# Two small matmul loops turned inside out, and the first two tiles of a projection interleaved, in a fused attention and MLP kernel

## The chip, the cores and the metric

The kernel runs on one core of one Trainium2 chip. The metric is the device time of one execution in microseconds (us). Runs count as fast or slow (slow here: over 1.5% above the fastest of the same kernel). One execution of each kernel is also taken by the hardware profiler, and its trace gives a start time for every instruction. PE is TensorE (matmuls), DVE is VectorE, ACT is ScalarE, POOL is GpSimd, SP issues DMAs.

## The reference, cut to what matters

```python
xn = layernorm(x)                                  # x: 2048 tokens x 1024
out = x + A(xn, mem0, Wq, Wk, Wv, Wo) + B(xn, w1, w2, w3, w4)

def B(x):                                          # the MLP branch
    h = gelu(layernorm(x) @ w1)
    ...                                            # shifts, w2, w3, w4

def A(x, mem0):                                    # 64 segments of 32 tokens, 8 memory rows
    for s in range(64):
        h = concat(mem, x[segment s])
        q, k, v = h @ Wq, h @ Wk, h @ Wv           # 32 heads of 128
        o = softmax(mask(q k^T / sqrt(128))) @ v @ Wo
        mem = o[:8]
        out.append(o[8:])
```

The kernel does not run the 64 segments one after another. It takes each segment's next memory from averages ("psvb" and "psG" below), computes all segments at once, and checks at the end that this was close enough; otherwise a serial branch recomputes.

## The kernel before

Three places matter. First, the start: tokens come in tiles of 128; a tile is normalised by VectorE, transposed on TensorE (the first ones) or by DMA (tile 4 and from tile 6 on), and multiplied by w1. The contraction has eight slices `k` of 128; w1 arrives in four loads of two slices each.

```python
load_x(0); load_x(1); load_w1(0); load_w1(2); load_x(2); load_w1(4); load_w1(6)
...
def w1_first(ks):                                  # tile 0: slice by slice, as w1 arrives
    for k in ks:
        for co in range(KT):
            nc.tensor.matmul(first[:, co // 4, co % 4, :], w1_sb[:, k, co * P:(co + 1) * P], xn2Ts[0][:, 0, k, :],
                             start=(k == 0 and co % 4 == 0), stop=(k == KT - 1), skip_group_check=True)

def single(n, b):                                  # other tiles: output by output
    ps = mm_tile("ps1")[:].rearrange("p (c t) -> p c t", c=4)
    for c in range(4):
        co = 4 * b + c
        for k in range(KT):
            nc.tensor.matmul(ps[:, c, :], w1_sb[:, k, co * P:(co + 1) * P], xn2Ts[n // 2][:, n % 2, k, :], ...)
    gelu4(n, b, ps)
...                                                # the order of issue
pe_trans(0); ln_half(1, 1)
w1_first(range(5))
load_segone(); load_eye9(); ln_half(2, 0); ln_apply(1)
pe_trans(1)
w1_first(range(5, KT))
for b in range(2): gelu4(0, b, first[:, b, :, :])
ln_half(2, 1); ln_apply(2)
single(1, 0); pe_trans(2); normalise_x(0); single(1, 1)
...
for g in range(2, NT // 2):                        # from tile 4 on, two tiles at a time, 256 columns
    for n in nxt:                                  # the next two tiles: 6 and 7 while 4 and 5 are multiplied
        ...
        ln_apply(n)
        dma_trans(n)                               # DMA transpose, issued by SP
    stage1(g, range(4))
    ...
    stage1(g, range(4, KT))
```

Second, eight small projections of averages (psvb, 63 columns) beside a third small product that is not touched (psG, 63 columns).

```python
MZ = cpool.tile([P, KT, NZ], BF16)                 # NZ = 71: rows 142 bytes apart
vbT = cpool.tile([P, H, NG], BF16)                 # NG = 63: rows 126 bytes apart
xb = spec.tile([P, KT, NG], BF16)
...
ps = aux_tile([P, 4, NG], "A", "psvb")
for hh in range(4):
    for k in range(KT):
        nc.tensor.matmul(ps[:, hh, :], w[:, k, hh * P:(hh + 1) * P], xb[:, k, :], start=(k == 0), stop=(k == KT - 1))
...                                                # psG: hh outer, k inner, output psG[:, k, :], moving operand vbT[:, c * 4 + hh, :]
```

Third, sixteen small projections of the memories (psM, 71 columns).

```python
def mem_proj(s, nm, dst):
    w = A[nm, s.i]
    ps = mm_tile("psM")
    p3_ = ps[:, 0:4 * NZ].rearrange("p (h z) -> p h z", h=4)
    for hh in range(4):
        for k in range(KT):
            nc.tensor.matmul(p3_[:, hh, :], w[:, k, hh * P:(hh + 1) * P], MZ[:, k, :], start=(k == 0), stop=(k == KT - 1))
    nc.scalar.copy(dst[:, hsl(s.hg), :], p3_)
```

In each matmul the second operand is the stationary one (the weights) and the third is the moving operand, which is streamed past it column by column.

Of the kernel before, what the change touches and what calls it, by code (L numbers as in the profile page):

```python
# [21 lines left out]
P = 128  # L22
S = 2048
D = 1024
KT = D // P
# [38 lines left out]
def kernel(  # L64
# [16 lines left out]
    nc = tc.nc  # L81
# [45 lines left out]
    MZ = cpool.tile([P, KT, NZ], BF16)  # L127
# [6 lines left out]
    def mm_tile(name):  # L134
        return psum.tile([P, 512], F32, tag="mm", bufs=4, name=name)

    def aux_tile(shape, tag, name):
        return psum.tile(shape, F32, tag=tag, bufs=1, name=name)
# [6 lines left out]
    xb = spec.tile([P, KT, NG], BF16)  # L145
# [18 lines left out]
    with ExitStack() as keepx:  # L164
# [6 lines left out]
        with ExitStack() as p0:  # L171
            big = p0.enter_context(tc.tile_pool(name="p0big", bufs=1))
            ring = p0.enter_context(tc.tile_pool(name="p0ring", bufs=3))
            w1_sb = big.tile([P, KT, D], BF16)
# [26 lines left out]
            def ln_half(n, c):  # L201
                if c == 0:
                    sts[n] = ring.tile([P, 2, 6], F32, tag="st", name="st")
                nc.vector.bn_stats(sts[n][:, c, :], xts[n][:, c * 512:(c + 1) * 512])
                if c == 0:
                    return
                nc.vector.bn_aggr(lnst[:, n, 0:2], sts.pop(n)[:])
                ab = ring.tile([P, 2], F32, tag="ab", name="ab")
                nc.vector.tensor_scalar(ab[:, 0:1], lnst[:, n, 1:2], EPS, None, op0=ALU.add)
                nc.vector.tensor_scalar(ab[:, 1:2], ab[:, 0:1], EPS, lnst[:, n, 1:2], op0=ALU.mult, op1=ALU.add)  # L210
                nc.gpsimd.tensor_tensor(lnst[:, n, 2:4], ab[:], neghalf[:], op=ALU.pow)
                for t in {0: (3,), 1: (4, 5), 2: (6, 7)}.get(n, (n + 5,)):
                    if t < NT:
                        load_x(t)

            def ln_stats(n):
                ln_half(n, 0)
                ln_half(n, 1)

            xn2Ts = {}  # L220
# [3 lines left out]
            def ln_apply(n):  # L224
                g, j = divmod(n, 2)
                if j == 0:
                    xn2Ts[g] = ring.tile([P, 2, KT, P], BF16, tag="xn2T", name="xn2T", bufs=4)
                xn2 = xn2s[n] = ring.tile([P, D], BF16, tag="xn2", name="xn2", bufs=4)
                nc.vector.tensor_scalar(xn2[:], xts[n][:], lnst[:, n, 0:1], lnst[:, n, 3:4], op0=ALU.subtract, op1=ALU.mult)
                nms[n] = ring.tile([P, 1], F32, tag="nm", name="nm", bufs=8)  # L230
                nc.gpsimd.tensor_scalar(nms[n][:], lnst[:, n, 0:1], lnst[:, n, 2:3], -1.0, op0=ALU.mult, op1=ALU.mult)
# [11 lines left out]
            def normalise_x(n):  # L243
                nc.scalar.activation(xts[n][:], xts[n][:], ACTF.Identity, bias=nms.pop(n)[:], scale=lnst[:, n, 2:3])

            def pe_trans(n):
                xn2 = xn2s.pop(n)
                ps = [mm_tile("psT")[:], mm_tile("psT")[:]]
                for h in range(2):
                    p3_ = ps[h].rearrange("p (k t) -> p k t", k=4)  # L250
                    for k in range(4):
                        nc.tensor.matmul(p3_[:, k, :], xn2[:, (4 * h + k) * P:(4 * h + k + 1) * P], ident[:], start=True, stop=True)
                    for q in range(0, 4, 2 if n == 0 else 4):
                        w = 2 if n == 0 else 4
                        nc.scalar.copy(xn2Ts[n // 2][:, n % 2, 4 * h + q:4 * h + q + w, :], p3_[:, q:q + w, :])
# [14 lines left out]
                for co in cos:  # L270
                    w1_part(g, co, mm_tile("ps1")[:, 0:256], range(KT))

            first = aux_tile([P, 2, 512], "B", "ps1")[:].rearrange("p b (c t) -> p b c t", c=4)

            def w1_first(ks):
                for k in ks:
                    for co in range(KT):
                        nc.tensor.matmul(first[:, co // 4, co % 4, :], w1_sb[:, k, co * P:(co + 1) * P], xn2Ts[0][:, 0, k, :],
                                         start=(k == 0 and co % 4 == 0), stop=(k == KT - 1), skip_group_check=True)

            def gelu4(n, b, ps):
                nc.scalar.activation(hTB[:, 4 * b:4 * b + 4, 2 + n * P:2 + n * P + P], ps, ACTF.Gelu_apprx_tanh)

            def single(n, b):
# [4 lines that stand above are left out]
                        nc.tensor.matmul(ps[:, c, :], w1_sb[:, k, co * P:(co + 1) * P], xn2Ts[n // 2][:, n % 2, k, :], start=(k == 0), stop=(k == KT - 1))  # L289
                gelu4(n, b, ps)  # L290
# [4 lines left out]
            ln_apply(0)  # L295
            pe_trans(0)
            ln_half(1, 1)
            w1_first(range(5))
            load_segone()
            load_eye9()  # L300
            ln_half(2, 0)
            ln_apply(1)
            pe_trans(1)
            w1_first(range(5, KT))
            for b in range(2):
                gelu4(0, b, first[:, b, :, :])
            ln_half(2, 1)
            ln_apply(2)
            single(1, 0)
            pe_trans(2)  # L310
            normalise_x(0)
            single(1, 1)
            ln_stats(3)
            ln_stats(4)
            ln_apply(3)
# [36 lines left out]
        with ExitStack() as p2:  # L352
            ring = p2.enter_context(tc.tile_pool(name="p2ring", bufs=4))
            for n in range(NT):
                x1 = ring.tile([P, D], F32, tag="x1", bufs=6)
                st = ring.tile([P, 2, 6], F32, tag="st")
                for ch in range(2):
                    ps = mm_tile("ps2")
# [25 lines left out]
    with ExitStack() as p3:  # L384
# [3 lines left out]
        for c in range(7):  # L388
            t = big.tile([P, 4, D], BF16, name=f"w4_{c}")
# [23 lines left out]
        def use_chunk(c):  # L413
            t = chunks.pop(c)
            if c < 8:
                w = t[:].rearrange("p (k e) -> p k e", k=KT)
                ps = aux_tile([P, 4, NG], "A", "psvb")
                for hh in range(4):
                    for k in range(KT):
                        nc.tensor.matmul(ps[:, hh, :], w[:, k, hh * P:(hh + 1) * P], xb[:, k, :], start=(k == 0), stop=(k == KT - 1))  # L420
                vb = vbT[:, c * 4:(c + 1) * 4, :]
                nc.vector.tensor_scalar(vb, ps[:], 1.0 / L, None, op0=ALU.mult)
                sq = ring.tile([P, 4, NG], F32, tag="sq", bufs=1, name="sq")
                nc.gpsimd.tensor_tensor(sq[:], vb, vb, op=ALU.mult)
                for hh in range(4):
                    if c == 0 and hh == 0:
                        nc.gpsimd.tensor_copy(thr[:], sq[:, 0, :])
                    else:
                        nc.gpsimd.tensor_tensor(thr[:], thr[:], sq[:, hh, :], op=ALU.add)
                if c == 7:  # L430
                    nc.gpsimd.tensor_scalar(chk[:, NV + 7:2 * NV], thr[:], TOL2, None, op0=ALU.mult)
                    nc.gpsimd.tensor_copy(chk[:, NV:NV + 7], chk[:, NV + 7:NV + 8].to_broadcast((P, 7)))
                return
            c -= 8
            w = t[:].rearrange("p (h d) -> p h d", h=4)
            if c == 0:
                psG[0] = aux_tile([P, KT, NG], "B", "psG")
            for hh in range(4):
                for k in range(KT):
                    nc.tensor.matmul(psG[0][:, k, :], w[:, hh, k * P:(k + 1) * P], vbT[:, c * 4 + hh, :],  # L440
                                     start=(c == 0 and hh == 0 and k == 0), stop=(c == 7 and hh == 3), skip_group_check=True)
            if c == 7:
                nc.vector.tensor_copy(MZ[:, :, M:NZ], psG[0][:])
# [100 lines left out]
        for tb in range(4):  # L544
            for f in range(FT):
                ps = mm_tile("ps3")
# [12 lines left out]
            for j in range(4):  # L559
                n = tb * 4 + j  # L560
# [3 lines left out]
                for ch in range(2):  # L564
                    ps = mm_tile("ps4")
# [20 lines left out]
    def hsl(hg):  # L586
        return slice(4 * hg, 4 * hg + 4)
# [53 lines left out]
    def mem_proj(s, nm, dst):  # L641
        w = A[nm, s.i]
        ps = mm_tile("psM")
        p3_ = ps[:, 0:4 * NZ].rearrange("p (h z) -> p h z", h=4)
        for hh in range(4):
            for k in range(KT):
                nc.tensor.matmul(p3_[:, hh, :], w[:, k, hh * P:(hh + 1) * P], MZ[:, k, :], start=(k == 0), stop=(k == KT - 1))  # L647
        nc.scalar.copy(dst[:, hsl(s.hg), :], p3_)

    def mem_cols(s):  # L650
# [191 lines left out]
    for i in range(NS):  # L842
        s = new_step(i)
        p = steps.get(i - 1)
# [72 lines left out]
        if last:  # L917
            b = s.b
# [35 lines left out]
    with tc.If(cond > 0):  # L954
        with ExitStack() as fctx:
# [17 lines left out]
            with tc.For_i(0, NSEG, 1) as i:  # L973
# [7 lines left out]
                for hg in range(8):  # L981
# [8 lines left out]
                    ps = fps.tile([P, 4, L], F32, tag="mm")  # L990
# [4 lines left out]
                    ps = fps.tile([P, 4, L], F32, tag="mm")  # L995
# [4 lines left out]
                    ps = fps.tile([P, 512], F32, tag="mm")  # L1000
# [33 lines left out]
                for ch in range(2):  # L1034
                    ps = fps.tile([P, 512], F32, tag="op")
# [44 lines left out]
```

## Time and profile before

| | before |
|---|---|
| time, median of 6 | 1503.70 us (1503.56 to 1504.64) |
| span of the profiled execution | 1502.0 us |
| PE busy | 1486.4 us, 99% |
| PE waits in the whole run | four, the last ends at 12.7 us |

The page of the kernel before, its busy times and the chain of work that ended last:

```profile
PE 1486.4 (99%) x9330; PEld 785.5 (52%) x9456; DVE 666.7 (44%) x1561; ACT 467.4 (31%) x1247; POOL 258.1 (17%) x707
...
PE 98%; DMA 1%; issue 0%; SPq 0%; DVE 0%
```

The waits of PE in the kernel before (who waited for whom: total us, times, longest):

```profile
PE ps L278 <- DMA w_sb<-in_B_w_dram: 1.5, 2, 0.9
PE psW L197 <- DVE fill L176: 1.5, 1, 1.5
PE psT L252 <- DVE xn L229: 1.2, 1, 1.2
PE ps L278 <- ACT xn2T L255: 0.2, 1, 0.2
```

PE is the bound, and after the start it never waits. So time can come from two places only: a shorter distance between the starts of matmuls, or the waits of the start-up. (After the last matmul come another 4.6 us, which the change does not touch.) The time order of PE in the kernel before (start, length, instruction; L278 is `w1_first`, L252 a transpose, L289 `single`; in brackets the idle time ahead and what ended it):

```profile
7.78 1.95 PE L278 MATMUL ps<-xn2T,w_sb 128*128 128x128 bf16 x32 [0.24 <-ACT xn2T L255]
10.64 0.62 PE L278 MATMUL ps<-xn2T,w_sb 128*128 128x128 bf16 x8 [0.92 <-DMA w_sb<-in_B_w_dram]
11.10 0.61 PE L252 MATMUL psT<-c_ident_sb,xn 128*128 128x128 bf16 x8
11.54 0.61 PE L278 MATMUL ps<-xn2T,w_sb 128*128 128x128 bf16 x8
12.71 1.07 PE L278 MATMUL ps<-xn2T,w_sb 128*128 128x128 bf16 x16 [0.56 <-DMA w_sb<-in_B_w_dram]
...
26.07 1.19 PE L265 MATMUL ps<-xn2T,w_sb 128*128 128x256 bf16 x9
```

Read it as: tile 0's first four slices, a wait for w1's third load, a transpose of tile 1, another wait for w1's fourth load. The first 128x256 matmul (L265, tiles 4 and 5) ends what is called the start-up below. The same view around the first psM group:

```profile
528.89 1.28 PE L647 MATMUL psM<-MZ,w 128*128 128x71 bf16 x32
530.01 2.32 PE L615 MATMUL psQ<-xm,w 128*128 128x512 bf16 x9
```

The lengths there include the last matmul's own latency (0.2 us), so the cost of a group is read from start to start: 530.01 - 528.89 = 1.12 us for 32 matmuls, 34.9 ns each. Single start times in the trace split this further: 31 to 32 ns after one matmul of each run of eight, 35 to 38 ns after the other seven.

### The profile page before, as it was taken

To read this page: it belongs to the slowest core of one execution; us is meant where nothing else is said; L and a number is where in the kernel's file an instruction comes from. 1 tells how busy PE (TensorE), PEld (TensorE's weight loads), DVE (VectorE), ACT (ScalarE), POOL (GpSimd) and SP (SyncE) were. 2 spreads that over 40 slices of the span, in tenths; PEclk is the share of its full clock that TensorE was granted. 3 is DMA by queue.
4 is the path that set the end of the run, shared out by engine and by line. 5 is a ranking of instruction groups with operands and counts; after the bars stand their busy time and mean duration, and the time that the engine had idled before them with its cause. 6 is when DMAs were issued, how large, how long until landed. Compare 5 with 4: busy or idle time off the path is not lost.

```text
span 1502.0 us, 23719 instructions
## 1 busy us (share of the span) xinstructions
PE 1486.4 (99%) x9330; PEld 785.5 (52%) x9456; DVE 666.7 (44%) x1561; ACT 467.4 (31%) x1247; POOL 258.1 (17%) x707
## 2 busy tenths in 40 slices
PE   8999999999999999999999999999999999999998
PEld 7844444444444466666644544444544544444544
DVE  8283010010110226666622777731676650576654
ACT  5633203103012035454501444420434430244420
POOL 6152131211110202121210111110111110111110
PEclk9999999999999999999999999999999999999999
DMA  7499753553121545474521454431455441344302
GB/s 223 131 276 219 269 186 99 184 175 132 63 92 42 197 136 188 142 224 141 183 71 61 140 168 141 155 103 49 141 152 158 141 132 58 104 138 141 118 0 72
DMA packets 189172, 208.11 MB, mean 139 GB/s; under 512 B 50168, under 2 KB 157832, under 8 KB 189056
## 3 DMA queue, kind: packets, MB, share of 16 engines
q1 hardware_dynamic: 180768, 178.82, 39.8%
q0 software_dynamic: 8288, 27.72, 5.2%
q8 instruction: 76, 1.25, 0.4%
q14 instruction: 40, 0.33, 0.1%
HBM read 170.07 MB, written 25.17 MB: 130 GB/s over the span
## 4 chain that ended last, share of the span: by engine, by line
PE 98%; DMA 1%; issue 0%; SPq 0%; DVE 0%
PE psK L631 15%; PE psQ L615 15%; PE psP L811 15%; PE psV L638 15%; PE ps L549 13%; PE ps L567 13%; PE ps L361 4%; PE ps L265 3%; PE psO L690 2%; PE psS L660 2%; PE psM L647 1%; PE ps L289 1%; DMA w_sb<-in_B_w_dram 1%; PE psvb L420 1%; PE psG L440 1%
## 5 line engine op out<-in xcount | busy, mean ns | idle before, releaser
L811 PE MATMUL psP<-wo_sb,oX 128*128 128x512 bf16 (+1 forms) x1036 | 221.7, 372 | 1.1
L664 ACT ACTIVATE ET<-psS 32x132 f32<-32x132 f32 x512 | 139.0, 271 | 203.7 <-PE psS L660 198.0
L567 PE MATMUL ps<-w,hT_all 128*128 128x512 bf16 x874 | 193.7, 379 | 1.2
L631 PE MATMUL psK<-xT,w 128*128 128x512 bf16 x747 | 176.3, 379 | 1.1
L615 PE MATMUL psQ<-xT,w 128*128 128x512 bf16 x750 | 175.8, 379 | 1.1
L638 PE MATMUL psV<-w,xT 128*128 128x512 bf16 x745 | 175.0, 379 | 1.0
L811 PEld LDWEIGHTS <-oX 128*128 128x128 bf16 x1056 | 102.8, 98 | 115.8
L631 PEld LDWEIGHTS <-w 128*128 128x128 bf16 x1280 | 121.2, 98 | 80.2
L550 ACT ACTIVATE hT_all<-ps 128x512 bf16<-128x512 f32 x112 | 66.7, 597 | 283.9 <-PE ps L549 283.9
L615 PEld LDWEIGHTS <-w 128*128 128x128 bf16 x1024 | 96.7, 98 | 104.2
L567 PEld LDWEIGHTS <-hT_all 128*128 128x128 bf16 x896 | 87.1, 98 | 103.9
L681 POOL TENSOR_TENSOR BD<-ET,c_segone_sb 128x16 bf16<-128x16 f32 x128 | 33.9, 265 | 491.1 <-ACT ET L664 491.1
L622 DVE TENSOR_TENSOR Q<-psQ,QM 128x512 bf16<-128x512 f32 (+1 forms) x128 | 85.6, 679 | 61.6 <-ACT Q L621 40.5
L638 PEld LDWEIGHTS <-xT 128*128 128x128 bf16 x768 | 72.0, 98 | 73.5
L666 DVE STREAM_TRANSPOSE EQ<-ET 128x128 f32<-128x128 f32 x128 | 39.9, 311 | 156.8 <-ACT ET L664 156.6
L639 ACT CAST V<-psV 128x512 bf16<-128x512 f32 x128 | 75.1, 586 | 110.1 <-PE psV L638 100.1
L632 ACT CAST K<-psK 128x512 bf16<-128x512 f32 (+1 forms) x160 | 80.3, 502 | 90.7 <-PE psK L631 88.9
L549 PE MATMUL ps<-xn3T,w3a 128*128 128x512 bf16 x448 | 97.7, 379 | 0.0
L549 PE MATMUL ps<-xn3T,w3b 128*128 128x512 bf16 x448 | 97.7, 379 | 0.0
L817 DVE TENSOR_TENSOR ot<-psP,Rt 128x512 bf16<-128x512 f32 (+1 forms) x33 | 22.2, 675 | 157.3 <-PE psP L811 157.3
L679 DVE TENSOR_TENSOR BD<-PT,c_segone_sb 128x512 bf16<-128x512 bf16 x128 | 90.0, 703 | 4.5
L694 DVE TENSOR_TENSOR oX<-psO,VM 128x512 bf16<-128x512 f32 (+1 forms) x128 | 86.3, 674 | 7.8 <-PE psO L690 7.8
(157 smaller groups left out, 1502.5 us busy)
## 6 DMA issues: line engine op xcount, KB each, us to landing
w<-in_A_Wq_dram SPq DMA_DIRECT2D x32, 1024.0 KB, 5.4
w<-in_A_Wk_dram SPq DMA_DIRECT2D x32, 1024.0 KB, 5.5
w<-in_A_Wv_dram SPq DMA_DIRECT2D x32, 1024.0 KB, 5.4
R_scratch<-x POOLq DMA_DIRECT2D x16, 512.0 KB, 7.9
R<-R_scratch SPq DMA_DIRECT2D x16, 512.0 KB, 7.1
chunk<-in_A_Wv_dram SPq DMA_DIRECT2D x8, 1024.0 KB, 5.6
R_scratch<-R POOLq DMA_DIRECT2D x16, 512.0 KB, 4.1
chunk<-in_A_Wo_dram SPq DMA_DIRECT2D x8, 1024.0 KB, 5.9
```

Of the source, the lines that this page charges most:

```text
L549: nc.tensor.matmul(ps[:], w3[:, k, (f % FH) * P:(f % FH + 1) * P], xn3Ts[tb][:, :, k, :], start=(k == 0), stop=(k == KT - 1))
L567: nc.tensor.matmul(ps[:], h3T[:, f, j * P:(j + 1) * P], w4t[f // 4][:, f % 4, ch * 512:(ch + 1) * 512], start=(f == 0), stop=(f == FT - 1))
L615: nc.tensor.matmul(ps[:], w[:, k, hh * P:(hh + 1) * P], s.xm[:, k, 0:512], start=(k == 0), stop=(k == KT - 1))
L622: nc.vector.tensor_tensor(q3[:, j0:16, 0:SEG], p3_[:, j0:16, :], QM[:, 4 * s.hg + hh, z + j0:z + 16].unsqueeze(2).to_broadcast((P, 16 - j0 ...
L631: nc.tensor.matmul(ps[:, 0:c], w[:, k, hh * P:(hh + 1) * P], s.xm[:, k, h2 * c:(h2 + 1) * c], start=(k == 0), stop=(k == KT - 1))
L632: nc.scalar.copy(s.K[:, hh, h2 * c:(h2 + 1) * c], ps[:, 0:c])
L638: nc.tensor.matmul(ps[:], s.xm[:, k, m * P:(m + 1) * P], w[:, k, :], start=(k == 0), stop=(k == KT - 1))
L639: nc.scalar.copy(s.V[:, m, :], ps[:])
L664: nc.scalar.activation(ET[q, :, :], ps[q, :, W * j:W * (j + 1)], ACTF.Exp, scale=SCALE)
L679: nc.vector.tensor_tensor(B4[:, :, :, 0:SEG], PT[:].unsqueeze(2).to_broadcast((P, 4, 4, SEG)), so.unsqueeze(3).to_broadcast((P, 4, 4, SEG) ...
L694: nc.vector.tensor_tensor(oX[:, hsl(s.hg), m * P:(m + 1) * P].rearrange("p h (j i) -> p h j i", i=SEG)[:, :, j0:4, :], p4[:, :, j0:4, 0:SE ...
L811: nc.tensor.matmul(ps[:, 0:w], oX[:, h, m * P:(m + 1) * P], wo_sb[:, h, cc], start=(h == 0), stop=(h == H - 1))
```

## The change

The intent: (1) in psvb and psM, go through the four heads inside the loop over the contraction, so that two consecutive matmuls never add to the same columns of PSUM, the memory in which TensorE sums; (2) at the start, put tile 1's first slices of w1 between those of tile 0, so that PE has work while w1 is still arriving.

The flag `start` has to move as well. The Trainium skill, "PSUM — Partial Sum Buffer", section "The four PSUM rules", says that a matmul with this flag clears the written-bits (which decide between adding and overwriting) of its whole bank, so that where several groups are open at once in a bank only the first matmul issued there may carry it. The new loops follow this.

```diff
-            w1_first(range(5))
+            w1_first(0, range(4))
             load_segone()
             load_eye9()
             ln_half(2, 0)
             ln_apply(1)
             pe_trans(1)
-            w1_first(range(5, KT))
-            for b in range(2):
-                gelu4(0, b, first[:, b, :, :])
+            w1_first(0, range(4, 6))
+            w1_first(1, range(3))
+            w1_first(0, range(6, KT))
             ln_half(2, 1)
             ln_apply(2)
-            single(1, 0)
+            w1_first(1, range(3, 6))
             pe_trans(2)
+            w1_first(1, range(6, KT))
             normalise_x(0)
-            single(1, 1)
 ... (w1_first takes the tile as an argument, keeps one PSUM tile for each, and issues the gelus after slice 7)
-                for hh in range(4):
-                    for k in range(KT):
-                        nc.tensor.matmul(ps[:, hh, :], w[:, k, hh * P:(hh + 1) * P], xb[:, k, :], start=(k == 0), stop=(k == KT - 1))
+                for k in range(KT):
+                    for hh in range(4):
+                        nc.tensor.matmul(ps[:, hh, :], w[:, k, hh * P:(hh + 1) * P], xb[:, k, :], start=(k == 0 and hh == 0),
+                                         stop=(k == KT - 1), skip_group_check=True)
 ... (mem_proj, psM: the same exchange of the two loops)
```

More of the change, by code (lines that the diff above doesn't have):

```diff
@@ L271, in stage1, with w1_first @@
                     w1_part(g, co, mm_tile("ps1")[:, 0:256], range(KT))
-            first = aux_tile([P, 2, 512], "B", "ps1")[:].rearrange("p b (c t) -> p b c t", c=4)
-            def w1_first(ks):
+            first = {}
+            def w1_first(n, ks):
+                if n not in first:
+                    first[n] = aux_tile([P, 2, 512], "BA"[n], "ps1")[:].rearrange("p b (c t) -> p b c t", c=4)
                 for k in ks:
                     for co in range(KT):
-                        nc.tensor.matmul(first[:, co // 4, co % 4, :], w1_sb[:, k, co * P:(co + 1) * P], xn2Ts[0][:, 0, k, :],
+                        nc.tensor.matmul(first[n][:, co // 4, co % 4, :], w1_sb[:, k, co * P:(co + 1) * P], xn2Ts[0][:, n, k, :],
                                          start=(k == 0 and co % 4 == 0), stop=(k == KT - 1), skip_group_check=True)
+                if ks[-1] == KT - 1:
+                    for b in range(2):
+                        gelu4(n, b, first[n][:, b, :, :])
             def gelu4(n, b, ps):
@@ L644, in mem_proj @@
         p3_ = ps[:, 0:4 * NZ].rearrange("p (h z) -> p h z", h=4)
-        for hh in range(4):
-            for k in range(KT):
-                nc.tensor.matmul(p3_[:, hh, :], w[:, k, hh * P:(hh + 1) * P], MZ[:, k, :], start=(k == 0), stop=(k == KT - 1))
+        for k in range(KT):
+            for hh in range(4):
+                nc.tensor.matmul(p3_[:, hh, :], w[:, k, hh * P:(hh + 1) * P], MZ[:, k, :], start=(k == 0 and hh == 0),
+                                 stop=(k == KT - 1), skip_group_check=True)
         nc.scalar.copy(dst[:, hsl(s.hg), :], p3_)
```

## The prediction

> **What bounds the kernel now.** TensorE. The page has PE busy 1486.4 of 1502.0 us (99%); the chain that ended last is 98% PE. The table of waits lists four PE waits in all, before 13 us: 1.5 us for the fill tile, 1.2 for the first normalised tile, 0.2 for ScalarE, 1.5 in two waits for w1's loads. Only shorter matmul pitches and those start-up waits can pay.
>
> **Part 1: small matmuls, contraction outermost.** 512 matmuls of 128x71 (psM) and 256 of 128x63 (psvb) change order. By start-to-start times in the trace, inside a run of eight that accumulates into the same columns psM has 35 to 36 ns, but 31 to 32 ns where the next matmul goes to another head's columns; a group of 32 takes 1.112 to 1.117 us (34.8 ns each). psvb: 32 against 28 to 29 ns, 1.009 us per group. psG (128x63) changes columns with every matmul already: 0.944 to 0.955 us per group, 29.6 ns. The Trainium skill, "TensorE: Matmul & The Clock Gate", section "Back-to-back issue gap", gives N/2.4 + 2.5 ns: 32.1 and 28.8, as at a column change (the 3 ns more on the same columns are in the trace alone). I expect psvb as psG: 8 x 0.06 = 0.5 us. For psM I put psG's surplus of 1.1 ns onto 31.7: about 32.7 ns, 1.045 us per group, 16 x 0.07 = 1.1 us. No PE wait lies near, so all 1.6 us is on the critical path. At 128x128 both orders have 55.8 ns already, so reordering w1 gains no pitch.
>
> **Part 2: tile 1's slices of w1 between tile 0's.** The work stays, 128 matmuls of 55.8 ns and two transposes of 0.45 us: 8.04 of the 9.86 us from tile 0's first matmul (7.775) to tile 2's first (17.632). The other 1.80 us are waits: 9.56 to 10.64 (w1's third load) and 11.99 to 12.71 (its fourth, landed 12.66). Now tile 1's transposes come before the fifth slice and wait only for VectorE's tile, done at 10.42: PE resumes about 10.48. From 10.94, 16 matmuls of tile 0 and 24 of tile 1 last until 13.17, past the landing of w1's last load, so the second wait goes. Tile 2's first matmul comes at about 16.75, 0.9 us earlier. ScalarE's second copy for tile 2 ends near 16.9, just as its fifth slice is wanted: perhaps 0.1 us is lost. Later inputs keep slack: transposed tile 4 landed at 24.29 (wanted about 25.2), tile 7 at 31.77 (about 32.7).
>
> **Sum.** 0.5 + 1.1 + 0.85 = about 2.5 us: **1501.5 us**. Range **1500.3 to 1502.8**. Faster by over 2%: 0.005; within 2%: 0.99; slower by over 2%: 0.005.
>
> **What would show it.** psM groups near 1.045 us and psvb near 0.95 by start times, with hardly any 35 (32) ns steps; psG unchanged. One PE wait of about 0.9 us (for VectorE's tile) between 9.5 and 10.5, none for w1's fourth load; the first 128x256 matmul at about 25.1 instead of 26.07; no PE wait after 17 us.
>
> **What would make it wrong.** If the 3 ns come from returning to the same columns within some 120 ns, a cycle of four heads may keep part of it (psG returns after eight). If changing the moving operand sets the pitch, it gains less. w1's loads may land later and eat part 2; ScalarE's copies, or a transposed tile landing after its new, earlier use, may hand the 0.9 us back as a new wait.

## The result, and the profile after

| | before | after |
|---|---|---|
| time, median of 6 | 1503.70 us | 1501.88 us (1501.19 to 1502.49) |
| ratio of fast runs | | 0.9987, 95% interval 0.9974 to 1.0 |
| span of the profiled execution | 1502.0 us | 1499.7 us |
| first 128x256 matmul | 26.07 us | 25.01 us |
| from it to the first psP matmul ("the stretch") | 731.33 us | 730.10 us |

A ratio is the mean time of one kernel's fast runs over that of the other's of the same rounds, so it is not quite the ratio of the medians quoted. The kernel is 1.8 us faster by medians, within 2%; the interval reaches 1, so the times alone do not settle the gain. All outputs are right.

The stretch is a yardstick for the rest of this text. It begins after the start-up and contains all psvb, psG and psM groups. In the seven profiles without padding (the benches, which add matmuls inside it, left out) it takes only two values, to 0.03 us: 731.33 us with the old loops and 730.10 to 730.13 with the new. What follows it, to the end, takes 744.5 to 744.6 us in every profile but the two with a delayed load, where it takes 744.1. So about 1.2 us of any difference is settled inside one profile, while the start-up varies from execution to execution, as will be seen.

The waits of PE in the kernel after:

```profile
PE psW L197 <- DVE fill L176: 1.5, 1, 1.5
PE psT L252 <- DVE xn L229: 1.5, 1, 1.5
PE ps L265 <- DMA xn2T<-xn: 0.3, 1, 0.3
PE ps L280 <- ACT xn2T L255: 0.2, 1, 0.2
```

Its time order of PE (L280 is `w1_first` now, and the end of the start-up is L265 as before):

```profile
7.97 1.95 PE L280 MATMUL ps<-xn2T,w_sb 128*128 128x128 bf16 x32 [0.24 <-ACT xn2T L255]
9.79 0.62 PE L252 MATMUL psT<-c_ident_sb,xn 128*128 128x128 bf16 x8
10.25 4.63 PE L280 MATMUL ps<-xn2T,w_sb 128*128 128x128 bf16 x80
...
16.05 1.95 PE L294 MATMUL ps<-xn2T,w_sb 128*128 128x128 bf16 x32
...
25.01 1.27 PE L265 MATMUL ps<-xn2T,w_sb 128*128 128x256 bf16 x10 [0.35 <-DMA xn2T<-xn]
```

No wait for w1 is left. But that is not yet proof of the new order, because w1 came earlier in this execution: its third load landed at 9.38 us (10.59 before) and its fourth at 10.74 (12.66 before), though SP issued them at the same times within 0.15 us, and ahead of everything that the change touches. Counted with 55.8 ns a matmul, the old order would not have waited for w1 here either: 7.97 + 144 x 0.0558 = 16.01 us for tile 2's first matmul, against 16.05 measured. And there is a new wait of 0.35 us, for tile 4, transposed by DMA; from start to start it cost 0.51 us (8.95 us from tile 2's first matmul to the first 128x256 one, against 8.44 before). So it is luck that the first 128x256 matmul came at 25.01 us, close to the 25.1 predicted. The predicted wait of 0.9 us for VectorE did not come either: tile 1 was normalised at 9.74 us, not 10.42, as tile 2's load, which VectorE's order takes first, landed at 8.02 us, not 9.26.

The first psM group after, start to start 1.07 us (528.46 - 527.39):

```profile
527.39 1.23 PE L653 MATMUL psM<-MZ,w 128*128 128x71 bf16 x32
528.46 1.89 PE L621 MATMUL psQ<-xm,w 128*128 128x512 bf16 x7
```

By single start times it is 33.1 ns a matmul: 31 to 33 ns for most, but still 34 to 40 ns for about every third. The trace shows which: on rows 1 to 7 of `MZ` the first of a row's four matmuls takes 35 to 40 ns every time, the middle two 31.9 and 31.8 on average, the last 33.6; on row 0 all four take 31.7 to 32.2 on average. psvb went from 31.5 to 29.9 ns, psG stayed at 29.6. So the groups did get shorter, by less than predicted in psM, and a rest of the slow steps stayed that the theory (adding to columns just added to) has no place for.

### The profile page after: what moved, and what is told of

Its sections match the earlier page's. It is cut to its first block, busy times and chain, and to the rows that moved or that the text cites. A ratio compares the mean times of both kernels' runs of the same rounds, so it can differ in the third digit from the quotient of the medians.

```text
span 1499.7 us, 23719 instructions
## 1 busy us (share of the span) xinstructions
PE 1484.9 (99%) x9330; PEld 784.3 (52%) x9456; DVE 666.2 (44%) x1561; ACT 466.8 (31%) x1247; POOL 257.4 (17%) x707
## 4 chain that ended last, share of the span: by engine, by line
PE 98%; DVE 1%; DMA 1%; issue 1%; POOL 0%; POOLq 0%
PE psK L637 15%; PE psP L818 15%; PE psQ L621 15%; PE psV L644 15%; PE ps L555 13%; PE ps L573 13%; PE ps L366 4%; PE ps L265 3%; PE psO L697 2%; PE psS L667 2%; PE psM L653 1%; PE psvb L425 1%; PE psG L446 1%; DVE st L204 0%; DMA xn2T<-xn 0%
```

## The experiments

Times of one paragraph are from the same chip and rounds, with runs of the kernel before between them. The 95% intervals of the ratios are 0.0013 to 0.0017 to either side, about 2 us, so times alone seldom decide here (of the experiments only pad_pe7's interval stays below 1); the profiles do.

### Each half alone, and the whole again

small_only is the kernel before with the psvb and psM loops of the diff; w1_only is the kernel before with the start-up part of the diff; after_again is the changed kernel unaltered.

Expected of small_only:

> The kernel before with only the psM and psvb loops reordered. My theory: 16 psM groups at 1.060 us and 8 psvb groups near 0.956 us as in the changed kernel, so 16 x 0.054 + 8 x 0.054 = 1.3 us less than before in time, whatever the start-up does: about 1502.4 us if before is 1503.7. In the profile the waits for w1's loads stay possible as in before. Rival (the gain is all from the start-up, where w1's loads happened to land 1.2 and 1.9 us earlier in the profile of after): under 0.4 us less than before.

Expected of w1_only:

> The kernel before with only tile 1's slices of w1 put between tile 0's. My theory after seeing both profiles: the gain is what the wait for w1's fourth load (and part of the third) would have been in that execution, and it shrinks where the loads land early, as they did in the profile of after (9.38 and 10.74 us against 10.59 and 12.66), and where the transposed tile 4 lands late (0.45 us lost there). So on average 0.3 to 0.8 us less than before, not the 0.85 of the prediction with certainty. Rival (the order of w1's slices is worth the whole 1.07 us by which the first 128x256 matmul moved between the two profiles): 0.9 to 1.1 us less. In the profile the psM groups are 1.114 us and psvb 1.009 again.

Expected of after_again:

> The changed kernel as it is, on the same chip as the two halves. If the halves add up, its gain over before is the sum of theirs within 0.4 us, in all 1.6 to 2.2 us. Second profile of the same start-up: if the landing of w1's loads varies from execution to execution, its landing times differ from 9.38 and 10.74 us by several tenths, and the wait for the transposed tile 4 is between 0 and 0.6 us.

| run | median us (before: 1504.09) | ratio, 95% | stretch us | w1's third, fourth load landed | tile 2's first matmul |
|---|---|---|---|---|---|
| small_only | 1502.59 | 0.9992, 0.9978 to 1.0005 | 730.13 | 10.37, 12.47 | 17.44 |
| w1_only | 1503.70 | 0.9993, 0.9979 to 1.0007 | 731.33 | 12.00, 13.20 | 17.86 |
| after_again | 1502.89 | 0.9988, 0.9974 to 1.0001 | 730.13 | 12.13, 13.44 | 17.99 |

The loop reordering is worth 731.33 - 730.13 = 1.2 us, and all of it: w1_only keeps the old stretch exactly. The start-up cannot be judged from these times. By medians the gains over before are 1.5, 0.4 and 1.2 us, so after_again missed its expectation (the sum of the halves within 0.4 us) by 0.3 us, well inside the noise. w1's loads landed up to 2.7 us apart between executions (9.38 in after, 12.13 in after_again), with the same DMAs issued in the same order. Where the third load is that late, the new order waits for it too. The time order of PE in w1_only:

```profile
7.88 1.07 PE L280 MATMUL ps<-xn2T,w_sb 128*128 128x128 bf16 x16 [0.24 <-DMA w_sb<-in_B_w_dram]
9.17 1.07 PE L280 MATMUL ps<-xn2T,w_sb 128*128 128x128 bf16 x16 [0.23 <-DMA w_sb<-in_B_w_dram]
11.01 0.62 PE L252 MATMUL psT<-c_ident_sb,xn 128*128 128x128 bf16 x8 [0.78 <-DVE xn L229]
12.04 4.64 PE L280 MATMUL ps<-xn2T,w_sb 128*128 128x128 bf16 x80 [0.41 <-ACT xn2T L255]
```

An estimate for the old order with the landings of w1_only: from 12.05 us, 8 + 8 + 8 + 16 + 64 + 8 matmuls of 55.8 ns follow without a gap, 18.30 us for tile 2's first, so the new order gains 0.44 us there; by the same sum 0.44 us in after_again.

### What makes a small matmul slow: groups of unread matmuls

bench is the changed kernel with groups of 32 matmuls put behind the first psM group. Their outputs are read by nobody. Each group stands behind three 128x512 matmuls, so that all begin alike, and each differs from one of psM's two loop orders in one thing.

```diff
         nc.scalar.copy(dst[:, hsl(s.hg), :], p3_)
+        if s.i == 0 and nm == "q":
+            bench(w, s.xm)
+    ...
+        run("bsame", n, f(HK))                       # heads outermost, as before; moving rows from MZ
+        run("brot", n, f(KH))                        # contraction outermost, as after
+        run("bpair", n, f(PAIR))                     # two heads in turn
+        run("bseven", n, ...)                        # seven places in turn
+        run("bover", n, ...)                         # heads outermost, start=True each time: overwrite, never add
+        run("bsamem", n, ...)                        # heads outermost, always MZ[:, 0] as moving operand
+        run("bsamew", n, ...)                        # heads outermost, always the same weights
+        run("brotm", n, ...); run("brotw", n, ...)   # contraction outermost with either held
+        run("bbanks", n, ..., tiles=4)               # contraction outermost, each head in its own bank
+        run("bsamex", n, f(HK), mv=xm)               # heads outermost, moving rows from xm, 1040 bytes apart
+        run("brotx", n, f(KH), mv=xm)                # contraction outermost, from xm
+        ... (both orders from xm at 32 to 128 columns)
```

> The changed kernel with groups of 32 unread matmuls put after the first psM group, each behind three 128x512 matmuls; only their start-to-start times are read, the total grows by some 60 us. At 71 columns: heads outermost 34.8 ns a matmul and contraction outermost 33.1, as in the kernels. My theory (surplus for adding to columns just added to): two heads in turn and seven places in turn are at or below 33.1; overwriting the same columns each time (no accumulation), a constant moving operand and a constant weight all keep 34 to 35 on the same columns if only the address matters; if accumulating matters, overwriting drops to 32. Rival A (the moving operand's change sets the pitch): a constant moving operand brings the same columns down to 32. Rival B (the weights' change does): constant weights bring them down to 32. The 35 to 39 ns steps that stay at contraction outermost vanish with seven places if they come from returning after four, with a constant moving operand if they come from its change, with constant weights if from the loads, and with four banks if from the shared bank. In the sweep of widths the surplus of the same columns is about 3 ns at 64 to 80 columns and gone at 128.

The time order of PE in bench (start, length; the tile's name tells the variant):

```profile
530.60 1.28 PE L671 MATMUL bsame<-MZ,w 128*128 128x71 bf16 x32
...
532.36 1.23 PE L671 MATMUL brot<-MZ,w 128*128 128x71 bf16 x32
...
537.51 1.28 PE L671 MATMUL bover<-MZ,w 128*128 128x71 bf16 x32
...
539.28 1.20 PE L671 MATMUL bsamem<-MZ,w 128*128 128x71 bf16 x32
...
540.96 1.28 PE L671 MATMUL bsamew<-MZ,w 128*128 128x71 bf16 x32
...
548.07 1.20 PE L671 MATMUL bsamex<-xm,w 128*128 128x71 bf16 x32
...
549.76 1.20 PE L671 MATMUL brotx<-xm,w 128*128 128x71 bf16 x32
```

Mean distance between starts, from the single start times in the trace (71 columns; a second pass of the twelve variants agreed within 0.1 ns):

```
heads outermost                                    34.8 ns
contraction outermost, four heads                  33.1
two heads in turn                                  33.8
seven places in turn                               33.3
heads outermost, overwriting instead of adding     34.9
heads outermost, same weights                      34.8
contraction outermost, same weights                33.2
contraction outermost, four banks                  33.1 (without two steps of 155 ns, 40.8 with them)
heads outermost, moving operand held               32.4
contraction outermost, moving operand held         32.4
heads outermost, moving rows from xm               32.4
contraction outermost, moving rows from xm         32.4
```

My theory fell here. Adding to the columns just added to costs nothing: bsamex does so in all but three of its steps and is as fast as any. Overwriting instead of adding changes nothing, nor do the weights or the bank. What does matter is the moving operand (in before, too, the short steps were those that read row 0, not those that change columns): hold it, or take it from another tile, and the loop order is worth nothing. In the widths from 32 to 128 columns, with xm as source, both orders agree within 0.2 ns (25.1 ns at 32, 29.1 at 64, 42.5 at 96, 55.8 at 128).

### Which property of the moving rows

bench2 reads 71 columns of one tile, xm, seen as one flat row, at starts of `k` times a chosen stride (heads outermost unless said).

```diff
+        flat = xm.rearrange("p k c -> p (k c)")
+        ...
+                nc.tensor.matmul(ps[:, hh * sl:hh * sl + n], w[:, k, hh * P:(hh + 1) * P], flat[:, o:o + n], ...)   # o = off(k)
+        for st in (71, 72, 76, 80, 96, 128, 520, 521, 522, 524, 528):
+            run("bst", NZ, by(st))
+        for c in (0, 1, 4, 8, 71):
+            run("bco", NZ, lambda k, c=c: c)           # held at one start
+        ...
```

> The first bench felled my theory: adding to the same columns costs nothing (32.4 ns both ways from another source tile, or with the moving operand held), so the surplus of 3 ns belongs to the moving operand MZ, whose rows lie 142 bytes apart. This bench reads 71 columns from one tile at chosen starts k x stride, heads outermost into the same columns. New theory (a switch to a row that starts off some alignment costs 3 to 4 ns): strides 71, 521, 522 elements (142, 1042, 1044 bytes) 34.8 ns, and 80, 96, 128, 528 at 32.4; where 72, 76, 520, 524 fall tells the alignment. Rival (rows that lie close together, as in one memory line): 71 to 128 elements all near 34.8 and 520 to 528 all 32.4. Held off alignment (constant starts at 2 and 142 bytes): 32.4 if the switch costs, 34.8 if every unaligned read does. Contraction outermost from stride 71 repeats the 33.1, from 72 or 521 as their alignment says. At 63 columns stride 63 gives 31.5 and stride 64 gives 28.7. At 128 and 260 columns no surplus if the longer stream hides it, 3 ns still if not.

The first two groups in the time order of PE, with strides of 142 and 144 bytes and the group behind each, 1.12 and 1.04 us from start to start:

```profile
531.05 1.27 PE L676 MATMUL bst<-xm,w 128*128 128x71 bf16 x32
532.17 0.81 PE L665 MATMUL bgap<-xm,w 128*128 128x512 bf16 x3
532.81 1.20 PE L676 MATMUL bst<-xm,w 128*128 128x71 bf16 x32
533.85 0.81 PE L665 MATMUL bgap<-xm,w 128*128 128x512 bf16 x3
```

Mean distance between starts, from the trace (bytes are twice the elements):

```
stride 142 bytes                    34.8 ns     held at 0 bytes      32.4 ns
stride 144 (9 x 16)                 32.4        held at 2            32.8
stride 152 (8 off a multiple of 16) 32.9        held at 8            32.5
stride 160, 192, 256                32.4        held at 16           32.4
stride 1040 (65 x 16)               32.4        held at 142          33.4
stride 1042                         33.1
stride 1044                         32.6        142, contraction outermost    33.2
stride 1048                         32.7        144, contraction outermost    32.4
stride 1056 (66 x 16)               32.4        1042, contraction outermost   32.9

63 columns: stride 126              31.7        stride 128           29.2
63 columns, contraction outermost   29.8        stride 128           29.1
96 columns, stride 194              44.8        (96 columns aligned: 42.5)
128 columns, stride 258             58.2        stride 1040          55.8
260 columns, stride 1042            111.7       stride 1040          110.8
```

Every stride that keeps the starts at multiples of 16 bytes gives the floor, and none of the others tried does. This fits what the Trainium skill, "SBUF — State Buffer", section "Specifications (TRN2)", says: lines of 16 bytes, with a penalty for each crossing to a new one. The number of lines alone does not give the cost, though: by an estimate from that line size a row held at 2 bytes lies in nine lines, as an aligned one does, and costs 0.4 ns; one held at 8 lies in ten and costs 0.1. How much an unaligned start costs depends on more: 2.4 ns where rows lie 142 bytes apart, 0.5 at 152, 0.2 to 0.7 where they lie over 1000 bytes apart, 0.1 to 1.0 for one row held. Starts that alternate between 2 and 1042 bytes, left out of the table, took 32.8, as one held at 2 did, so a change of row need not cost more by itself; 70 and 72 columns at 142 bytes took 34.1 and 35.1. So both theories of the expectation were only half right: alignment decides whether there is a cost, and the pattern of the starts how much. Why the pattern matters stays open (142 and 1042 bytes give the same eight remainders by 16, in opposite order). It does suggest how the reordering gained: it holds each unaligned row for four matmuls, of which the middle two are as fast as aligned ones in the profile of after, and a held row costs less than a changing one (33.4 against 34.8 at 142 bytes).

### The cure: rows padded to a multiple of 32 bytes

```diff
-    MZ = cpool.tile([P, KT, NZ], BF16)
-    vbT = cpool.tile([P, H, NG], BF16)
+    MZ_t = cpool.tile([P, KT, 80], BF16)
+    MZ = MZ_t[:, :, 0:NZ]
+    vbT_t = cpool.tile([P, H, 64], BF16)
+    vbT = vbT_t[:, :, 0:NG]
...
-    xb = spec.tile([P, KT, NG], BF16)
+    xb_t = spec.tile([P, KT, 64], BF16)
+    xb = xb_t[:, :, 0:NG]
```

pad_before is the kernel before with this alone, pad_after the changed kernel with this, and pad_start is pad_after with a different start: VectorE's `ln_half(2, 0)`, which waits for tile 2's load, moved behind `pe_trans(1)`, and tile 1's slices 0 to 3 ahead of tile 0's slice 4.

> The kernel before, loops and order unchanged, with the rows of MZ 80 elements apart instead of 71 and those of xb and vbT 64 instead of 63, so that every row of a moving operand starts at a multiple of 32 bytes. Theory (the surplus is the unaligned start of the moving rows): psM 32.4 ns a matmul heads outermost (34.9 before, 33.1 in the changed kernel), psvb and psG 29.1 (31.6 and 29.6); the stretch from the first 128x256 matmul to the first psP matmul, 731.33 us in before and 730.13 in the changed kernel, becomes 731.33 - 512 x 2.4 ns - 256 x 2.4 ns - 256 x 0.5 ns = about 729.4. Time 1.9 us below before, more than the loop reordering alone gains. Rival (it is the number of heads in turn after all, and the other bench tile was special): psM stays near 34.8.

> The changed kernel with the same padding. Theory: with aligned rows the loop order no longer matters, so psM 32.4, psvb and psG 29.1 as in pad_before and the same stretch of 729.4 us; time below the changed kernel by 0.35 + 0.2 + 0.1 = about 0.7 us, and below before by 1.9 us plus what the w1 order gains at these landings (0 to 0.9).

> The candidate that should beat both: pad_after, with VectorE normalising tile 1 ahead of tile 2's first statistics (which wait for tile 2's own load, landed at 8.0 to 10.1 us) and tile 1's first four slices of w1 ahead of tile 0's fifth. TensorE's wait for tile 1 should end near 9.8 us instead of 11.0 to 11.3, and tile 2's first matmul should start at 16.5 to 16.8 us whatever the landing of w1's third and fourth loads up to 12.5 and 14 us, against 17.6 to 18.0 in the profiles with usual landings and 16.05 in the one with early ones. The transposed tile 4, landed at 24.3 to 25.4 us, is wanted near 25.0, so up to 0.4 us can be lost there. Time 2.5 to 3.2 us below before.

| run | median us (before: 1503.84) | ratio, 95% | psM, psvb, psG ns | stretch us | third, fourth load landed | tile 2's first matmul |
|---|---|---|---|---|---|---|
| pad_before | 1503.36 | 0.9998, 0.9985 to 1.0012 | 32.4, 29.1, 29.1 | 729.46 | 10.21, 12.29 | 17.27 |
| pad_after | 1502.50 | 0.9991, 0.9977 to 1.0005 | 32.4, 29.1, 29.1 | 731.00 | 10.27, 12.40 | 16.41 |
| pad_start | 1502.70 | 0.9993, 0.9979 to 1.0006 | 32.4, 29.1, 29.2 | 729.47 | 10.50, 12.49 | 17.10 |

The first psM group of pad_before in the time order of PE, with the old loop order, is the shortest of all kernels, 1.03 us from start to start:

```profile
527.82 1.20 PE L650 MATMUL psM<-MZ_t,w 128*128 128x71 bf16 x32
528.85 2.32 PE L618 MATMUL psQ<-xm,w 128*128 128x512 bf16 x10
```

The stretch of 729.46 us was forecast at 729.4. So padding alone, with the loops as they were, takes 1.87 us from the stretch where the reordering took 1.2, and with padding the loop order is worth nothing. That unaligned rows cause the surplus is shown; why the chip charges it is not.

These profiles also give the fair comparison of the two start-ups, since the loads landed within 0.11 us of each other: tile 2 starts at 16.41 us in the new order and at 17.27 in the old, 0.85 us, which is what the prediction's second part claimed. A second pair agrees: 16.62 us in pad_after_again (landings 10.48 and 12.51) against 17.44 in small_only (10.37 and 12.47). pad_start missed: it starts tile 2 at 17.10, not 16.5 to 16.8, because PE waited 0.5 us for ScalarE's copies of tile 1's transpose and 0.3 us for those of tile 2's; its median is 1.1 us below before, not 2.5 to 3.2.

But the times did not follow. pad_before's median is 0.5 us below before where the stretch promises 1.9, and its ratio of 0.9998 shows no gain in the whole time; its profiled execution took 1501.59 us, the other four 1503.27 to 1504.17. And the stretch of pad_after is 1.5 us too long. Its waits of PE say why:

```profile
PE psT L255 <- DVE xn L232: 1.7, 2, 1.3
PE psW L200 <- DVE fill L179: 1.5, 1, 1.5
PE ps L268 <- DMA xn2T<-xn: 1.4, 1, 1.4
PE ps L283 <- ACT xn2T L258: 0.2, 1, 0.2
```

The third line is the DMA transpose of tile 7, landed at 33.68 us, 7.3 us after its issue; PE was ready for it at about 32.3. Padding is not needed for this: the profile of bench2, the changed kernel's start without padding, has a wait of 1.32 us for tile 7 as well (landed at 34.22 us).

### The late tile

pad_pe7 is pad_after with tile 7 transposed on TensorE; pad_after_again is pad_after once more, on the same chip.

```diff
-                    dma_trans(n)
+                    if n != 7:
+                        dma_trans(n)
                 stage1(g, range(4))
+                if g == 2:
+                    pe_trans(7)
```

> pad_after with tile 7 transposed on TensorE (8 matmuls, 0.45 us) instead of by DMA. In the profile of pad_after TensorE waited 1.5 us for that tile's DMA (landed 33.68 us, wanted at 32.3); in pad_before, w1_only and after it did not, yet the timed runs of both padded kernels fell 1 to 2 us short of what the stretch of 729.47 us promises. Theory (a late landing of tile 7 is what eats it in most runs): no PE wait after 26 us, stretch 729.47 + 0.45 = 729.9 us, times within 0.7 us of each other near 1501.2, that is 1.2 us below pad_after on the same chip. Rival (the shortfall lies elsewhere, in the first 25 us or the last matmuls): no faster than pad_after, rather 0.3 us slower, and the spread stays.

> pad_after unchanged, for the same chip as pad_pe7 and a second profile. Near 1502.5 us; a wait for the transposed tile 7 of 0 to 2 us in the profile, and the stretch from the first 128x256 matmul to the first psP matmul 729.47 us plus that wait.

| run | times us | median (before: 1504.21) | ratio, 95% | stretch us |
|---|---|---|---|---|
| pad_pe7 | 1501.00, 1501.93, 1501.51, 1502.49, 1502.70 | 1501.93 | 0.9984, 0.9969 to 0.9998 | 729.88 |
| pad_after_again | 1505.19, 1502.49, 1502.01, 1504.14, 1503.38 | 1503.38 | 0.9989, 0.9975 to 1.0003 | 733.74 |

(One of the nine executions of before in these rounds took 2646.07 us. It is not among the fast runs, no profile was taken of it, and its cause is not known; the record gives it a mean granted clock of 0.556. Without it the median of before is 1504.01.)

In pad_pe7 PE waits for nothing after 10 us, and the stretch is what was forecast. Its median is the furthest below before of all kernels here, 2.1 us (from 1504.01), and 1.45 us below pad_after_again on the same chip; that is less than the spread of single runs, and it is not shown to be faster than the changed kernel (ratios 0.9984 against 0.9987 and 0.9988, with intervals that overlap). Its times still spread by 1.7 us, not the 0.7 expected, so the late tile is not the only thing that varies.

pad_after_again shows the accident at its worst. Its time order of PE:

```profile
29.00 3.65 PE L268 MATMUL ps<-xn2T,w_sb 128*128 128x256 bf16 x32
35.09 5.32 PE L268 MATMUL ps<-xn2T,w_sb 128*128 128x256 bf16 x32 [2.44 <-DMA xn2T<-xn]
```

A group of 32 takes 3.65 us ahead of the wait and 5.32 us after it. The table of windows of the same run has the cause in its third column from the right, the granted clock (us; busy time and count of each engine; clock; DMA share; GB/s):

```profile
core 0: us, PE busy (x) PEld busy (x) DVE busy (x) ACT busy (x) POOL busy (x), PEclk, DMA share, GB/s
26.00:32.00 6.00, 6.00 (x70) 5.41 (x68) 5.79 (x16) 5.25 (x11) 4.71 (x8) 1.00 1.12 133
...
36.00:37.00 1.00, 1.00 (x6) 0.74 (x5) 1.00 (x2) 0.39 (x1) 0.71 (x2) 0.50 0.97 338
37.00:38.00 1.00, 1.00 (x7) 0.70 (x5) 0.90 (x5) 0.00 (x0) 0.14 (x1) 0.50 1.14 308
...
39.00:41.00 2.00, 2.00 (x32) 1.82 (x31) 1.17 (x5) 0.94 (x4) 0.85 (x3) 0.97 1.02 234
```

0.6 us after PE resumed from 2.44 us of idleness the clock fell to half, for 3.41 us; the matmuls' starts lie 213 ns apart there instead of 109. The 4.3 us by which this stretch exceeds 729.47 are the wait (2.6 us from start to start) and some 1.7 us of half clock.

### The last load of w1 made late on purpose

late_before and late_after are the two kernels with one more load of 0.5 MB in front of w1's fourth.

```diff
             load_w1(4)
+            nc.sync.dma_start(w2_sb[:, 0:2, :], w2_v[:, 0:2, :])
             load_w1(6)
```

> The kernel before with one more load of 0.5 MB (a part of w2, loaded again later) ahead of w1's fourth load, so that this lands 1 to 2 us later, near 14 us. TensorE then waits for it after tile 0's sixth slice of w1, so tile 2's first matmul starts 16 + 64 matmuls and a transpose, 4.9 us, after the landing: near 19 us. Later than before by the delay of the landing. Partner of late_after.

> The changed kernel with the same extra load. My theory (tile 1's first three slices, 24 matmuls of 55.8 ns = 1.34 us, run while the fourth load is awaited): tile 2's first matmul starts 3.6 us after a landing that is late enough, 1.3 us sooner than late_before in time from the landing, and the time is 1.2 us (psM and psvb) plus about 1.3 us below late_before, less what the transposed tile 4 takes back. Rival (reordering w1 gains nothing, the start-up of after was only luck): 1.2 us below late_before.

| run | median us (before: 1503.99) | ratio, 95% | fourth load landed | tile 2's first matmul | from landing to it |
|---|---|---|---|---|---|
| late_before | 1507.01 | 1.0015, 0.9998 to 1.0031 | 16.53 | 23.13 | 6.6 us |
| late_after | 1504.27 | 1.0003, 0.9986 to 1.0020 | 15.91 | 19.54 | 3.6 us |

The stretch differs by 1.2 us between them (731.33 and 730.13), and the medians by 2.7 us. late_after took the 3.6 us expected from the landing: the 24 matmuls of tile 1 did fill the wait. late_before took 6.6 instead of 4.9, and the rest is the clock once more, as the windows of late_before show (the first ends with the wait):

```profile
14.00:16.50 2.50, 0.06 (x2) 0.00 (x0) 2.40 (x7) 0.50 (x2) 1.47 (x4) 1.00 0.60 208
...
19.00:20.00 1.00, 1.00 (x12) 1.00 (x11) 0.93 (x4) 0.00 (x0) 0.83 (x3) 0.50 0.34 131
```

Here PE had been idle for 2.51 us, and the half clock came 1.35 us after it resumed and lasted 3.41 us. In late_after it was idle for 1.78 us and its clock did not fall. The fourteen traces together say more. Each has a fall after its last matmul, two have one before it too, and all sixteen falls come a whole number of times 3.413 us after the clock first became full (4 times in late_before, 9 in pad_after_again, 437 to 458 at the ends). Cut into such stretches, the sixteen that end in a fall had PE idle for 2.03 to 3.41 us (by the trace's modelled ends), the 6152 others for 1.90 us at most. This rule is read off afterwards; no run was made to test it. The Trainium skill, "TensorE: Matmul & The Clock Gate", section "What's actually happening", has the half rate set in after at least one idle window of about 3.4 us; the half rate and the length agree, but a stretch that was idle for 2.03 us of its 3.41 was enough.

## Why the prediction was right or wrong

- **The bound, and the total: right, the total partly by luck.** PE is at 99%, 1501.88 us is near the 1501.5 predicted, and the gain of 1.8 us by medians is a little under the 2.5 forecast. But the loops gained 1.2 of their 1.6 us for another reason than the one given, and in the profile of after the start-up came out as forecast because the loads landed early.
- **psvb: right in size.** 31.5 to 29.9 ns, 8 groups x 0.054 us = 0.4 us against 0.5.
- **psM: mis-sized.** "About 32.7 ns, 1.045 us per group, 16 x 0.07 = 1.1 us" became 33.1 ns, 1.060 us, 0.87 us by the groups. "Hardly any 35 (32) ns steps" was wrong: about every third step stayed slow.
- **The cause of the 3 ns: wrong.** The prediction put them on adding to "the same columns". bench shows no such cost; they belong to moving rows that do not start at a multiple of 16 bytes, and pad_before removes them with the loops untouched. It also read its trace one step off: the 31 to 32 ns lie not "where the next matmul goes to another head's columns" (35 ns) but after the matmul that reads row 0 of `MZ`, the only one of the eight rows that lies a multiple of 16 bytes from the tile's start. That the new order gained at all is luck: it happens to change the unaligned row a quarter as often. The prediction had named a change of the moving operand among the things that would make the gain smaller, which is close to what happened.
- **The order of w1's slices: right where the loads land as in the profile of before, not in general.** "0.9 us earlier" is 0.85 us between pad_before and pad_after. It is about 0.4 us (an estimate) where the third load is late, nothing where both are early, as in the profile of after, and about 1.3 us against the landing, clock apart, where only the fourth is late. The prediction took one execution's landings for the kernel's.
- **"Later inputs keep slack": wrong.** Tile 4 was wanted about 0.7 us earlier than forecast and landed 0.67 later in the profile of after, and PE lost 0.5 us to it there, 0.35 of them idle (in after_again it landed 1.1 us ahead of its use). PE waited for tile 7 in two profiles of the padded kernels, by 1.4 and 2.4 us, and in bench2, by 1.3. The prediction had listed this as a risk; in the two profiles of the changed kernel itself tile 7 was in time.

What stays open: why tile 6's and tile 7's transposes land when they do (tile 6 landed at 29.2 to 30.5 us in the five padded profiles, at 27.8 to 30.6 in the seven unpadded ones without a delayed load, so padding does not explain it); what held back pad_before's other four executions, which have no trace; and how the cost of an unaligned row comes to depend on the rows around it.

## What to carry to other kernels

When a small matmul is slower than another of its size, look at the address of its moving operand before its loop order: rows padded so that each starts at a multiple of 16 bytes (32 here) took 1.87 us from the stretch where the reordering took 1.2, and made it needless, though no whole time is precise enough to show the difference. A wait at the start-up is worth what the landing times make it in that execution, so compare orders at equal landings, or delay the load on purpose. Work that starts earlier runs into the next input sooner; check what each following DMA has to spare, since a wait of 2.4 us brought 1.7 us of half clock with it.

## What the Trainium skill lacked or had wrong

- "TensorE: Matmul & The Clock Gate", "Back-to-back issue gap": N/2.4 + 2.5 ns, which the section gives for a matmul on its own, fits aligned moving rows in these groups (32.1 against 32.4 ns at 71 columns, 42.5 against 42.5 at 96), but the section does not say that an unaligned moving row adds up to 2.5 ns (34.8 ns at 71 columns, 31.7 at 63, 58.2 instead of 55.8 at 128).
- "SBUF — State Buffer", "Specifications (TRN2)": has the 16-byte lines, but no cost for TensorE's moving operand. Measured: nothing at multiples of 16 bytes, 0.1 to 2.4 ns a matmul of 71 columns otherwise.
- "TensorE: Matmul & The Clock Gate", "What's actually happening": the table asks for at least one idle window of about 3.4 us. Here a stretch of 3.413 us with 2.03 us or more without a matmul ended in the half clock, sixteen times of sixteen, and none with 1.90 us or less did; the two spells inside the runs lasted 3.41 us.
- "DMA: Bandwidth & Descriptors": a spread of landing times would have helped. The same load, issued at 3.17 us in each profile, landed between 9.38 and 12.18 us in the seven unpadded profiles without a delayed load; tile 7's DMA transpose took 4.8 to 8.4 us from issue to landing.
